# Output projection of a fused recurrence and gated MLP: weights held still, gated tile streamed, sums block-transposed on the way out

## The chip, the cores and the metric

The kernel runs on one NeuronCore of one Trainium2 chip. The metric is the device time of one launch in microseconds, the median of several runs. Five engines matter. TensorE multiplies 128x128 blocks: it loads one operand, the stationary one, into its array, and streams the other, the moving one, past it; the sums land in PSUM. VectorE and ScalarE do elementwise work, GpSimd does almost nothing here, and SyncE's queue issues every DMA. Each engine works through its own instructions in the order in which they were written, and waits on semaphores for the others.

## The reference, cut to what matters

Inputs q, k, v, a_re and a_im have the shape (4, 8, 768, 48): batches, heads, time steps, head dimension. The first half is a linear recurrence with a complex decay per channel, the second a gated MLP over its output:

```python
mag = np.sqrt(a_re * a_re + a_im * a_im)
scale = np.minimum(mag, 0.999) / (mag + 1e-06)
for t in range(S):                                # S_re, S_im: 48x48 states per batch and head
    new_re = ar * S_re - ai * S_im                # ar, ai: a_re, a_im of step t, times scale
    new_im = ar * S_im + ai * S_re
    S_re, S_im = (new_re + kv, new_im)            # kv: outer product of k[t] and v[t]
    y[:, :, t] = einsum('bhd,bhde->bhe', q[:, :, t], S_re)
x = y.transpose(0, 2, 1, 3).reshape(3072, 384)
g = x @ w_gate                                    # 384 x 1536
out = (g * sigmoid(g) * (x @ w_val)) @ w_out      # 1536 x 384
```

The weights arrive as 64-bit floats, everything else as 32-bit floats.

## The kernel before, in words

Tokens are cut into 24 slabs of 128 rows, and two slabs form a group of 256 tokens (12 groups, numbered 0 to 11). For each group `stage_ops` (L364) computes decays and phases of both slabs on ScalarE and VectorE, `slab_ops` (L590) turns the recurrence of a slab into matmuls on keys and queries that were rotated and scaled by these, and `ffn_ops` (L912) runs the gated MLP. From slab 6 on the keys and queries are turned by VectorE's 32x32 block transposes (L637) and brought into place by twelve small DMAs for each slab (L646, tile `T`); `sc` (L679, tile `p_ps`) is the first product of a slab that needs them.

The MLP has 12 steps for each group, one for each 128 columns of the hidden dimension. A step is written `g.f`. `f1` (L927) makes the gate and value columns in PSUM (`p_gv`); `th` (L933, ScalarE) applies silu; `h2` (L938, VectorE) multiplies by the value, giving `sg`, 128 hidden columns by 256 tokens. From group 1 on TensorE works on rounded 32-bit operands, so that each number is split in a high and a low part: `hh` is the rounded `sg`, `hl` what is left (L340). Three products high*high, high*low and low*high make up one. `f1` thus has 18 matmuls with 256 streamed columns each (two matrices, three blocks of the contraction, three products).

`f2` (L961) multiplies by the output weights. Before the change the gated tile is stationary, 128 tokens at a time, and the 384 weight columns stream: two halves of tokens by three products, 6 matmuls of 384 columns, each half summed over the 12 steps in a PSUM tile of its own (`p_po`, one bank each). The sums have tokens on partitions. `oe` (L972) copies each half to SBUF (`ost`), on ScalarE or VectorE as it falls, and `os` (L975) stores it with one DMA of 128 rows. Group 0 differs: it works on unsplit 32-bit numbers.

The weights are turned from 64-bit words into 32-bit floats by three VectorE operations (`c1` to `c3`), then split into high (`c4`, on ScalarE or VectorE) and low (`c5`); `w` in these names stands for the gate and value weights, `o` for the output weights.

The order of all this is made by a planner at build time (`Planner.plan`, L110). Each operation has an estimated cost, a due time, its dependences and the buffers that it holds, and the planner deals the operations out to the engines one after another, by due time and by constants (L32 to L53). What it writes is the order of each engine's instructions; on the chip only semaphores hold. The names in the change are those of the planner's operations: `h2_2.3`, `oe3.0`, `evt010` (eviction of a TensorE transpose), `kl`, `k1`, `k2` (range checks of the weights), `kz`, `km` (range checks of the decays), `tr` (block transposes), `sh` (the twelve DMAs).

Of the kernel before, what the change touches and what calls it, by code (L numbers as in the profile page):

```python
# [33 lines left out]
SWITCH_KEY = 8.903  # L34
RUSH, WARY = 100.0, 8.0
CALM_S, CALM_C, CALM_T, CALM_A, CALM_D = 4.319, 1.268, 0.639, 0.272, 0.3
LATE, WARY2, WARY3, WARY4 = 2.18, 1.96, 1.727, 0.007
STRETCH = 1.757
AHEAD, YIELD, QUEUED = -15.937, 12.575, 8.752
T0, PER, FT, FT0 = 49.251, 22.663, 4.032, 4.936  # L40
LEAD0, LEAD2 = 12.884, 2.091
CONV0, CONVP = 32.474, 43.543
T1 = T0 + 12 * FT0
CK0, CKP = 169.077, 13.465
RCP, SQR = 1, 2

# [3 lines left out]
TURN_OVER, STILL, GATED, INPUT = 128, 96, 16, 16  # L50
HIGH, LOW, WHOLE = 0, 1, 2
SHY = -4.043
POOL_FROM = 9.827  # L53
# [17 lines left out]
class Planner:  # L71
# [29 lines left out]
    def urge(self):  # L101
# [119 lines left out]
def quick(ctx, tc, q, k, v, a_re, a_im, w_gate, w_val, w_out, out, count):  # L221
# [4 lines left out]
    still = ctx.enter_context(tc.tile_pool(name="still", bufs=1))  # L226
    gap = ctx.enter_context(tc.tile_pool(name="gap", bufs=1))
# [22 lines left out]
    still.tile([P, STILL], F32, name="ahead")  # L250
    gap.tile([P, TURN_OVER - STILL], F32, name="behind")
# [3 lines left out]
    def place(nm, f, dtype):  # L255

        pool = still if nm == "w" else work
        return pool.tile([P, 2 * WIDE[nm]], dtype, name=f"w{nm}{f}", tag=f"w{nm}{f}", bufs=1)

    def spare(nm):  # L260
# [4 lines left out]
        return W[nm]  # L265

# [44 lines left out]
    def new(tag, inst):  # L311
# [4 lines left out]
        elif tag in PSUMS:  # L316
            t = psum.tile([P, 512], F32, name="p_" + tag, tag=tag, bufs=2 if tag == "po" else slots[tag])
# [483 lines left out]
    def weight_ops(f):  # L801
        for nm, n, user in (("w", 2 * DM, "f1"), ("o", DM, "f2")):
# [37 lines left out]
            def c4(e, nm=nm, n=n, whole=whole):  # L840
                W.pop((nm, f - 1, WHOLE), None)
                W[nm, f] = place(nm, f - 1, F32R)
                cast(e, W[nm, f][:, 0:n], whole())

            def c5(e, nm=nm, n=n, whole=whole):
                tt(e, W[nm, f][:, n:2 * n], whole(), W[nm, f][:, 0:n].bitcast(F32), ALU.subtract)
# [65 lines left out]
    def ffn_ops(g):  # L912
        t0, step = (T1 + (g - 1) * NF * FT, FT) if g else (T0, FT0)
        for f in range(NF):
# [36 lines left out]
            def f2(e, f=f, I=I):  # L951
                hh, hl, h = (at_.get((x, I)) for x in ("hh", "hl", "sg"))
                products = ((hh, HIGH), (hh, LOW), (hl, HIGH)) if g else ((h, WHOLE),)
                if f == 0:
                    new("po", f"{g}.0")
                    new("po", f"{g}.1")
                for i in range(2):
                    cs = slice(i * P, (i + 1) * P)
                    po = at_["po", f"{g}.{i}"][:, :DM]
                    for j, (l, part) in enumerate(products):  # L960
# [261 lines left out]
```

## Time and profile before

| | us |
|---|---|
| median of 3 runs | 633.49 |
| the runs | 632.08, 633.49, 633.57 |
| the profiled execution's own time | 632.41 |
| its span, from first to last instruction | 630.7 |
| TensorE matmuls busy in it | 599.1 |
| VectorE busy | 502.6 |
| ScalarE busy | 399.3, of this table loads 146.3 |

The granted clock was 0.998 of 2.4 GHz over the span. A busy TensorE in this profile is one that has a matmul in flight: the ends are modelled, so the pace of matmuls is read from the distance of their starts, and idle time from windows and waits.

### The profile page before, as it was taken

How to read it: one execution, taken by the hardware profiler on the slowest of the kernel's cores; microseconds unless marked ns; L12 is line 12 of the kernel's file. 1: busy time of each engine (PE TensorE's matmuls, PEld its weight loads, DVE VectorE, ACT ScalarE, POOL GpSimd, SP SyncE). 2: the span in 40 equal slices, each digit the busy share in tenths (PEclk: the TensorE clock that was granted, in tenths of full speed). 3: DMA queues.
4: the chain of work that ended last, by engine and by line, in shares of the span. 5: the costliest groups of instructions: out<-in, count | busy, mean ns of one | idle time of the engine just before them, and what ended most of it. 6: DMA issues, size and time to landing. Idle time of an engine off the chain costs nothing.

```text
span 630.7 us, 16366 instructions
## 1 busy us (share of the span) xinstructions
PE 599.1 (95%) x6690; PEld 562.8 (89%) x6690; DVE 502.6 (80%) x930; ACT 399.3 (63%) x650; POOL 4.2 (1%) x15
## 2 busy tenths in 40 slices
PE   2779999989899999999999999999999999999996
PEld 1467788979899999999999999999999999999995
DVE  8999999998986978977989869869879958544432
ACT  7864238886776885767876966966966854221211
POOL 2000000000000000000000000000000000000000
PEclk9999999999999999999999999999999999999999
DMA  8899601233655465555365553563553551431200
GB/s 263 239 294 302 201 27 32 65 120 95 156 134 134 119 133 127 130 144 135 88 146 137 140 135 90 133 167 95 131 164 97 138 151 45 128 81 46 76 1 30
DMA packets 155575, 79.91 MB, mean 127 GB/s; under 512 B 116187, under 2 KB 151261, under 8 KB 155494
## 3 DMA queue, kind: packets, MB, share of 16 engines
q1 hardware_dynamic: 155494, 78.80, 46.4%
q8 instruction: 54, 0.88, 0.6%
q14 instruction: 27, 0.22, 0.1%
HBM read 59.83 MB, written 4.78 MB: 102 GB/s over the span
## 4 chain that ended last, share of the span: by engine, by line
PE 76%; DVE 14%; ACT 3%; SPq 3%; issue 2%; DMA 2%; DVEq 0%
PE p_gv L927 39%; PE p_po L961 20%; PE p_py L679 6%; PE p_ps L679 6%; PE p_pm L745 2%; PE p_pm L491 2%; DVE ww L340 2%; SPq L646 2%; PE p_gv L617 1%; ACT L1053 1%; DVE sg L938 1%; DVE ks L340 1%; DVE s L340 1%; DMA re<-in_a_re_dram 1%; ACT s L395 1%
## 5 line engine op out<-in xcount | busy, mean ns | idle before, releaser
L927 PE MATMUL p_gv<-xh,ww 128*128 128x256 f32 x1596 | 303.0, 287 | 4.1 <-DVE sg L938 3.5
L927 PEld LDWEIGHTS p_gv<-xh,ww 128*128 128x128 f32 x1596 | 255.9, 189 | 12.2 <-DVE sg L938 5.7
L927 PE MATMUL p_gv<-xl,ww 128*128 128x256 f32 x726 | 201.2, 277 | 0.0
L1053 ACT ACT_TABLE_LOAD x114 | 146.3, 1283 | 2.1
L933 ACT ACTIVATE sg<-p_gv 128x256 f32<-128x256 f32 x144 | 54.5, 384 | 130.4 <-PE p_gv L927 129.1
L927 PEld LDWEIGHTS p_gv<-xl,ww 128*128 128x128 f32 x726 | 136.3, 188 | 0.1
L961 PE MATMUL p_po<-wo,hh 128*128 128x384 f32 x484 | 125.5, 340 | 0.0
L938 DVE TENSOR_TENSOR sg<-sg,p_gv 128x256 f32<-128x256 f32 x144 | 59.0, 414 | 62.5 <-ACT sg L933 62.3
L961 PEld LDWEIGHTS p_po<-wo,hh 128*128 128x128 f32 x484 | 81.2, 188 | 2.4 <-issue 2.2
L961 PE MATMUL p_po<-wo,hl 128*128 128x384 f32 x242 | 80.8, 334 | 0.0
L340 DVE TENSOR_TENSOR hl<-sg,hh 128x256 fp32r<-128x256 f32 x132 | 54.5, 418 | 5.3 <-ACT hh L344 0.8
L961 PEld LDWEIGHTS p_po<-wo,hl 128*128 128x128 f32 x242 | 45.4, 188 | 0.0
L395 ACT ACTIVATE s<-s 128x768 f32<-128x768 f32 x44 | 37.0, 844 | 11.2 <-DVE s L340 7.2
L679 PEld LDWEIGHTS p_ps<-T 96*64 96x64 f32 x768 | 35.9, 138 | 5.9 <-issue 2.9
L679 PE MATMUL p_ps<-T 96*64 96x128 f32 (+1 forms) x768 | 39.6, 254 | 0.9 <-DVE T L346 0.9
L344 ACT CAST hh<-sg 128x256 fp32r<-128x256 f32 x49 | 19.8, 405 | 22.5 <-DVE sg L938 20.2
L707 DVE TENSOR_TENSOR sc<-p_ps,turn 128x512 f32<-128x512 f32 x48 | 32.0, 687 | 2.5 <-PE p_ps L679 2.1
L346 DVE CAST hh<-sg 128x256 fp32r<-128x256 f32 x83 | 23.8, 289 | 3.7 <-PE p_po L961 0.4
L679 PE MATMUL p_py<-sc,vr 128*32 128x128 f32 x384 | 26.4, 273 | 0.0
L884 ACT ACTIVATE wo<-wo 128x384 f32<-128x384 f32 x36 | 20.1, 560 | 9.0 <-DMA wo<-in_moe_w_gate_dram 6.3
L765 ACT CAST xh<-p_py 128x384 fp32r<-128x384 f32 x22 | 10.5, 479 | 23.4 <-PE p_py L679 23.2
L679 PE MATMUL p_py<-sc,vt 128*32 128x128 f32 x384 | 25.0, 273 | 0.0
(140 smaller groups left out, 853.1 us busy)
## 6 DMA issues: line engine op xcount, KB each, us to landing
T<-ww SPq DMA_DIRECT2D x216, 64.0 KB, 2.9
wo<-in_moe_w_out_dram SPq DMA_DIRECT2D x24, 384.0 KB, 6.1
ww<-in_moe_w_gate_dram SPq DMA_DIRECT2D x12, 384.0 KB, 5.9
vt<-in_v_dram SPq DMA_DIRECT2D x24, 192.0 KB, 4.0
ww<-in_moe_w_val_dram SPq DMA_DIRECT2D x12, 384.0 KB, 6.7
out_dram<-ost SPq DMA_DIRECT2D x24, 192.0 KB, 2.4
wo<-in_moe_w_gate_dram SPq DMA_DIRECT2D x12, 384.0 KB, 3.7
wo<-in_moe_w_val_dram SPq DMA_DIRECT2D x12, 384.0 KB, 3.4
```

Of the source, the lines that this page charges most:

```text
L340: V[e].tensor_tensor(out=out, in0=a, in1=b, op=op)
L344: nc.scalar.copy(out=out, in_=in_)
L346: nc.vector.tensor_copy(out=out, in_=in_)
L395: nc.scalar.activation(out=of(dst), in_=of(source), func=func, scale=scale, **kw)
L679: nc.tensor.matmul(out=o, lhsT=l, rhs=r, start=opens, stop=closes, tile_position=(0, width * slot), skip_group_check=True)
L707: nc.vector.tensor_tensor(out=s.rearrange("p (r m) t -> p r m t", m=2), in0=scores[qd].rearrange("p (r m) t -> p r m t", m=2), in1=m, op=A ...
L884: nc.scalar.activation(out=high(0), in_=high(1), func=AF.Square, accum_out=flags[:, fl_hi + j:fl_hi + j + 1])
L927: nc.tensor.matmul(out=gv[:, i, :], lhsT=l, rhs=r, start=(m == 0), stop=(m == len(mm) - 1))
L933: nc.scalar.activation(out=new("sg", I), in_=at_["gv", I][:, 0:2 * P], func=AF.Silu)
L938: nc.vector.tensor_tensor(out=sg, in0=sg, in1=at_["gv", I][:, 2 * P:4 * P], op=ALU.mult)
L961: nc.tensor.matmul(out=po, lhsT=l[:, cs], rhs=weight("o", f, part), start=f == 0 and j == 0, stop=f == NF - 1 and j == len(products) - 1)
L1053: nc.scalar.preload_act_table_set(op.load)
```

## The change

In groups 1 to 10 `f2` now loads the output weights as the stationary operand, 128 output columns at a time, and streams the whole gated tile, 256 tokens: three blocks of output columns by three products, 9 matmuls of 256 columns. The sums have output columns on partitions and 256 tokens along the row, 768 floats in one PSUM tile of two banks. `oe` turns them back by one VectorE transpose of 32x32 blocks for each slab. A block transpose leaves the four blocks of a column of blocks where they are, so the split of the output weights (`c4`, `c5`) writes their columns in another order (`rows_of`), and the store takes four DMAs for each slab, in runs of 96 floats, where it took one. Groups 0 and 11 (`upright`) keep the former products; group 11 undoes the column order in its copy. The PSUM tile `po` is one tile with two banks instead of two tiles with one. Two padding tiles are gone, and the gated tiles and inputs start 48 floats into their buffers instead of 16. The planner has other constants, and a table that moves single due times.

```diff
-SWITCH_KEY = 8.903
+SWITCH_KEY = 3.7845
+NUDGE = {
+    "sadd0.1": -5.6, "lnr1": 0.2, "cumF1.1": 3.8, "mk1_2": 14.3, "mk1_3": 15.5, "c32w": 4.0, "c110w": 3.4,
...
-TURN_OVER, STILL, GATED, INPUT = 128, 96, 16, 16
+TURN_OVER, GATED, INPUT = 128, 48, 48
...
+        for op in self.ops:
+            op.key += NUDGE.get(op.name, 0.0)
...
+    def rows_of(nm, at, plain=False):
+        if nm != "o":
+            return at
+        return at.rearrange("p (q k m) -> p q k m", k=KT, q=4) if plain else at.rearrange("p (k q m) -> p q k m", k=KT, q=4)
...
-            t = psum.tile([P, 512], F32, name="p_" + tag, tag=tag, bufs=2 if tag == "po" else slots[tag])
+            t = psum.tile([P, 1024 if tag == "po" else 512], F32, name="p_" + tag, tag=tag, bufs=slots[tag])
...
-                cast(e, W[nm, f][:, 0:n], whole())
+                cast(e, rows_of(nm, W[nm, f][:, 0:n]), rows_of(nm, whole(), True))
...
+        upright = g in (0, NGRP - 1)
...
-                    for j, (l, part) in enumerate(products):
-                        nc.tensor.matmul(out=po, lhsT=l[:, cs], rhs=weight("o", f, part),
-                                         start=f == 0 and j == 0, stop=f == NF - 1 and j == len(products) - 1)
...
+                wh, wl = (weight("o", f, x).rearrange("p (k n) -> p k n", k=KT) for x in (HIGH, LOW))
+                for k in range(KT):
+                    for j, (l, r) in enumerate(((wh, hh), (wl, hh), (wh, hl))):
+                        nc.tensor.matmul(out=po[:, 2 * P * k:2 * P * k + 2 * P], lhsT=l[:, k, :], rhs=r,
+                                         start=f == 0 and j == 0 and k != 1, stop=f == NF - 1 and j == 2, skip_group_check=True)
...
-                cast(e, new("ost", I), at_["po", I][:, :DM])
+                    cast(e, *((rows_of("o", x, plain) for x, plain in ((o, True), (part, False))) if g else (o, part)))
+                else:
+                    nc.vector.transpose(out=o.rearrange("p (j k m) -> p k j m", j=4, k=KT),
+                                        in_=po[:, 0:2 * P * KT].rearrange("p (k i j m) -> p k i j m", k=KT, i=2, j=4)[:, :, i])
...
+                for q in range(4):
+                    nc.sync.dma_start(out=r.rearrange("(j a) (q n) -> q a j n", a=32, q=4)[q],
+                                      in_=o[32 * q:32 * q + 32].rearrange("a (j n) -> a j n", j=4))
```

On TensorE, where group 5 ends and group 6 begins, the order before had this, from the last matmul of `f1` 6.2 on (`hh` and `hl` of step 6.0 are stationary, two PSUM tiles):

```order
L927 MATMUL p_gv_4668<-xh_4272,ww1_919 128x256
L961 MATMUL p_po_4698<-wo-1_298,hh_4663 128x384 x2
L961 MATMUL p_po_4698<-wo-1_298,hl_4687 128x384
L961 MATMUL p_po_4699<-wo-1_298,hh_4663 128x384 x2
L961 MATMUL p_po_4699<-wo-1_298,hl_4687 128x384
L927 MATMUL p_gv_4716<-xh_4272,ww2_941 128x256
```

After the change the same place reads (the first operand named is the moving one, `wo` is stationary):

```order
L941 MATMUL p_gv_5598<-xh_5091,ww1_904 128x256
L980 MATMUL p_po_5632<-hh_5594,wo-1_336 128x256 x2
L980 MATMUL p_po_5632<-hl_5596,wo-1_336 128x256
L980 MATMUL p_po_5632<-hh_5594,wo-1_336 128x256 x2
L980 MATMUL p_po_5632<-hl_5596,wo-1_336 128x256
L980 MATMUL p_po_5632<-hh_5594,wo-1_336 128x256 x2
L980 MATMUL p_po_5632<-hl_5596,wo-1_336 128x256
L941 MATMUL p_gv_5648<-xh_5091,ww2_934 128x256
```

Six matmuls of 384 columns have become nine of 256, in the same place between the same two steps of `f1`.

On VectorE, in group 2 (`sg` rows are `h2`, the product by the value columns; `hl` rows the low parts; `ks`, `qs` and the transposes belong to the next slabs), the order before had, from `h2_2.1` on:

```order
L938 TENSOR_TENSOR sg_1860<-sg_1860,p_gv_1802 128x256
L340 TENSOR_TENSOR ks_1871<-kt_1362,s1_1821 128x16x48
L340 TENSOR_TENSOR qs_1601<-qt_1373,s1_1821 128x16x48
L340 TENSOR_TENSOR hl_1902<-sg_1792,hh_1823 128x256
L340 TENSOR_TENSOR ks_1871<-kt_1362,s3_1437 128x16x48
L340 TENSOR_TENSOR qs_1601<-qt_1373,s3_1437 128x16x48
L637 STREAM_TRANSPOSE ww11_1451<-ks_1871 128x4x2x3x32
L938 TENSOR_TENSOR sg_1916<-sg_1916,p_gv_1833 128x256
L637 STREAM_TRANSPOSE ww11_1451<-qs_1601 128x4x2x3x32
L340 TENSOR_TENSOR hl_1948<-sg_1860,hh_1900 128x256
```

and after the change, with the two transposes of group 1's sums (`ost`) around `h2_2.1`:

```order
L996 STREAM_TRANSPOSE ost_1900<-p_po_1091 128x3x4x32
L952 TENSOR_TENSOR sg_1875<-sg_1875,p_gv_1828 128x256
L996 STREAM_TRANSPOSE ost_1908<-p_po_1091 128x3x4x32
L353 TENSOR_TENSOR ks_1932<-kt_1372,s1_1847 128x16x48
L952 TENSOR_TENSOR sg_1910<-sg_1910,p_gv_1879 128x256
L353 TENSOR_TENSOR ks_1932<-kt_1372,s3_1455 128x16x48
L353 TENSOR_TENSOR qs_1616<-qt_1386,s1_1847 128x16x48
L650 STREAM_TRANSPOSE ww11_1467<-ks_1932 128x4x2x3x32
L353 TENSOR_TENSOR qs_1616<-qt_1386,s3_1455 128x16x48
L353 TENSOR_TENSOR hl_1980<-sg_1875,hh_1934 128x256
L650 STREAM_TRANSPOSE ww11_1467<-qs_1616 128x4x2x3x32
L952 TENSOR_TENSOR sg_1995<-sg_1995,p_gv_1912 128x256
```

Between `h2_2.1` and `h2_2.2` there were four products of 768 columns, one `hl` and a transpose of 768; now there are one transpose of 384 and one product of 768. The `hl` of step 2.0 has moved up, ahead of the rows shown.

On SyncE's queue, around slab 10 (`T` rows are the DMAs that bring keys and queries in place, `out_dram` the store of group 3), the order before had:

```order
L646 DMA T<-ww_1451 32x8x64 x3
L668 DMA vr_89<-in_v_dram 64x2x48 x4
L654 DMA vt_87<-in_v_dram 128x8x48
L646 DMA T<-ww_1451 32x8x64 x9
L975 DMA out_dram<-ost 128x384 x2
L537 DMA s_3384<-fr 128x768
```

and after the change:

```order
L659 DMA T<-ww_1467 32x8x64 x3
L681 DMA vr_83<-in_v_dram 64x2x48 x4
L1005 DMA out_dram<-ost 32x4x96 x4
L659 DMA T<-ww_1467 32x8x64 x9
L1005 DMA out_dram<-ost 32x4x96 x4
L550 DMA s_3539<-fr 128x768
```

Four stores stand ahead of the nine `T` DMAs, where one load of `v` stood, which has moved behind them.

## Rows read from the trace of the kernel before

**Rows 1.** The page's first part: busy time, share of the span, instructions.
```profile
PE 599.1 (95%) x6690; PEld 562.8 (89%) x6690; DVE 502.6 (80%) x930; ACT 399.3 (63%) x650; POOL 4.2 (1%) x15
```

**Rows 2.** Windows: stretch, length, busy time of each engine, granted clock, DMA share, GB/s.
```profile
0.00:45.00 45.00, 26.73 (x284) 16.97 (x284) 41.34 (x67) 33.58 (x55) 4.18 (x15) 1.00 0.86 268
45.00:131.00 86.00, 84.42 (x653) 71.09 (x652) 85.93 (x158) 49.14 (x75) 0.00 (x0) 1.00 0.43 121
131.00:175.00 44.00, 39.92 (x518) 36.80 (x516) 41.06 (x66) 34.65 (x56) 0.00 (x0) 1.00 0.47 136
175.00:624.00 449.00, 447.49 (x5237) 437.70 (x5237) 333.67 (x641) 281.50 (x465) 0.00 (x0) 1.00 0.45 114
624.00:630.70 6.70, 0.53 (x4) 0.20 (x2) 0.56 (x1) 0.48 (x1) 0.00 (x0) 0.80 0.20 67
```

**Rows 3.** Chain of work that ended last, 396 to 412 us: start, length, what.
```profile
398.70 2.06 PE p_gv L927 x18
400.76 1.04 PE p_po L961 x6
...
```

**Rows 4.** The chain, 421 to 432 us.
```profile
425.12 0.35 PE p_pm L491 x2
425.47 2.04 PE p_gv L927 x18
...
```

**Rows 5.** Groups by line: names, shapes, count, busy us, mean ns, idle before.
```profile
L1053 ACT ACT_TABLE_LOAD x114 | 146.3, 1283 | 2.1
...
L637 DVE STREAM_TRANSPOSE ww<-ks 128x768 f32<-128x768 f32 x18 | 17.5, 974 | 3.3 <-DMA T<-ww 3.1 <-DMA out_dram<-ost 0.2
...
L346 DVE COPY ost<-p_po 128x384 f32<-128x384 f32 x13 | 7.0, 550 | 1.2 <-PE p_po L961 1.2
...
L346 DVE COPY T<-p_gv 96x512 f32<-96x512 f32 x6 | 4.1, 684 | 0.4 <-PE p_gv L617 0.3
...
L346 DVE CAST ww<-ww 128x768 fp32r<-128x768 f32 x4 | 2.3, 571 | 0.0
```

**Rows 6.** Timeline of VectorE, 163 to 177 us: start, length, instruction.
```profile
165.10 0.41 DVE L938 TENSOR_TENSOR sg<-sg,p_gv 128x256 f32<-128x256 f32 x1
165.43 0.95 DVE L340 TENSOR_TENSOR ks<-kt,s 128x768 f32<-128x768 f32 x1
...
170.13 0.39 DVE L938 TENSOR_TENSOR sg<-sg,p_gv 128x256 f32<-128x256 f32 x1
...
175.02 0.75 DVE L938 TENSOR_TENSOR sg<-sg,p_gv 128x256 f32<-128x256 f32 x2
```

**Rows 7.** Waits of TensorE, 158 to 178 us: total us, times, longest.
```profile
PE p_gv L927 <- DVE sg L938: 2.4, 3, 1.6
```

**Rows 8.** Tile `p_po`, 355 to 360 us: duration min/median/max ns, first and last start.
```profile
L961 PE MATMUL p_po<-wo-1_298,hh x4: 335/338/339, 358.8 to 359.5; 128*128 128x384 f32 x4
...
L961 PE MATMUL p_po<-wo,hl x2: 331/332/333, 356.1 to 356.6; 128*128 128x384 f32 x2
L346 DVE COPY ost<-p_po x2: 549/550/551, 357.3 to 357.7; 128x384 f32<-128x384 f32 x2
```

**Rows 9.** Timeline of SyncE's queue, 258 to 276 us.
```profile
260.08 1.97 SPq L646 DMA_DIRECT2D T<-ww  x3
...
265.50 6.80 SPq L646 DMA_DIRECT2D T<-ww  x9
272.40 1.03 SPq L975 DMA_DIRECT2D out_dram<-ost  x2
```

**Rows 10.** The chain, 272 to 280 us.
```profile
276.71 1.55 PE p_ps L679 x24
```

**Rows 11.** The page's DMA issues: names, count, KB each, median us to landing.
```profile
T<-ww SPq DMA_DIRECT2D x216, 64.0 KB, 2.9
```

**Rows 12.** Timeline of all engines, 622 to 631 us.
```profile
624.04 0.56 DVE L346 COPY ost<-p_po 128x384 f32<-128x384 f32 x1 [1.22 <-PE p_po L961]
...
624.56 0.48 ACT L344 COPY ost<-p_po 128x384 f32<-128x384 f32 x1 [3.06 <-PE p_po L961]
625.07 1.09 SPq L975 DMA_DIRECT2D out_dram<-ost  x2
```

More of the change, by code (lines that the diff above doesn't have):

```diff
@@ L33 @@
 HOP = 0.189
-SWITCH_KEY = 8.903
+SWITCH_KEY = 3.7845
 RUSH, WARY = 100.0, 8.0
-CALM_S, CALM_C, CALM_T, CALM_A, CALM_D = 4.319, 1.268, 0.639, 0.272, 0.3
-LATE, WARY2, WARY3, WARY4 = 2.18, 1.96, 1.727, 0.007
+CALM_S, CALM_C, CALM_T, CALM_A, CALM_D = 4.0404, 0.9631, 0.2445, 0.2607, 0.2775
+LATE, WARY2, WARY3, WARY4 = 2.1401, 1.7581, 1.3142, 0.0
 STRETCH = 1.757
[L39 to L42, printed above, removed]
+AHEAD, YIELD, QUEUED = -15.9216, 13.0405, 5.6794
+T0, PER, FT, FT0 = 49.2709, 22.6488, 4.035, 4.9297
+LEAD0, LEAD2 = 8.0784, 1.9836
+CONV0, CONVP = 33.0252, 40.2957
 T1 = T0 + 12 * FT0
-CK0, CKP = 169.077, 13.465
+CK0, CKP = 169.2028, 13.465
 RCP, SQR = 1, 2
+NUDGE = {
[9 rows of a table added]
+}
 WIDE_KEYS = 64
 TURNS = P // WIDE_KEYS
-TURN_OVER, STILL, GATED, INPUT = 128, 96, 16, 16
+TURN_OVER, GATED, INPUT = 128, 48, 48
 HIGH, LOW, WHOLE = 0, 1, 2
-SHY = -4.043
-POOL_FROM = 9.827
+SHY = -9.7365
+POOL_FROM = 9.8301
 TABLES = {"exp": ("exp_and_others", "natural_log_exp_and_others"), "ln": ("natural_log_exp_and_others",),
@@ L249, in quick @@
     turned_v = [const.tile([P, 2, 2, 64], F32, name=f"vr{i}") for i in range(2)]
-    still.tile([P, STILL], F32, name="ahead")
-    gap.tile([P, TURN_OVER - STILL], F32, name="behind")
     W, HALVES = {}, {}
@@ L255, in place @@
     def place(nm, f, dtype):
-        pool = still if nm == "w" else work
-        return pool.tile([P, 2 * WIDE[nm]], dtype, name=f"w{nm}{f}", tag=f"w{nm}{f}", bufs=1)
+        return work.tile([P, 2 * WIDE[nm]], dtype, name=f"w{nm}{f}", tag=f"w{nm}{f}", bufs=1)
     def spare(nm):
@@ L952, in f2 @@
                 hh, hl, h = (at_.get((x, I)) for x in ("hh", "hl", "sg"))
-                products = ((hh, HIGH), (hh, LOW), (hl, HIGH)) if g else ((h, WHOLE),)
                 if f == 0:
[L955 to L959, printed above, removed]
-                    for j, (l, part) in enumerate(products):
-                        nc.tensor.matmul(out=po, lhsT=l[:, cs], rhs=weight("o", f, part),
-                                         start=f == 0 and j == 0, stop=f == NF - 1 and j == len(products) - 1)
+                    new("po", g)
+                po = at_["po", g]
+                if upright:
+                    products = ((hh, HIGH), (hh, LOW), (hl, HIGH)) if g else ((h, WHOLE),)
+                    for i in range(2):
+                        for j, (l, part) in enumerate(products):
+                            nc.tensor.matmul(out=po[:, 512 * i:512 * i + DM], lhsT=l[:, P * i:P * i + P], rhs=weight("o", f, part),
+                                             start=f == 0 and j == 0, stop=f == NF - 1 and j == len(products) - 1)
+                    return
+                wh, wl = (weight("o", f, x).rearrange("p (k n) -> p k n", k=KT) for x in (HIGH, LOW))
[3 more added lines that the diff above has]
+                                         start=f == 0 and j == 0 and k != 1, stop=f == NF - 1 and j == 2, skip_group_check=True)
             PO = [("po", g)]
```

18 lines of the change are left out of this document (11 added, 7 removed), and 8 rows, old and new, of the table NUDGE.

## Prediction, made before the changed kernel ran

> **What bounds the kernel now.** I read the page's first part, then windows, then the chain of waits inside them, then the groups by line. TensorE has a matmul in flight 95% of the span [rows 1], but the windows show four regimes [rows 2]. Up to 45 us TensorE is busy 26.7 of 45, and VectorE 41.3: the start-up of decays and phases. From 45 to 131 us both are full (84.4 and 85.9 of 86), so there a gain on one is worth something only with the other. From 131 to 175 us TensorE lacks 4.1 us and VectorE 2.9. From 175 to 624 us TensorE is busy 447.5 of 449 while VectorE is idle a quarter of the time: whatever shortens TensorE's instructions there comes off the end one for one, and nothing that VectorE, ScalarE or the queue does matters until TensorE waits for it. The last 6.7 us are the final copy, the store and the closing. The granted clock was 1.00 in the first four stretches [rows 2], the upper level, 2.4 GHz.
>
> **The products, part by part.** One step is 6 x 384 = 2304 streamed columns before and 9 x 256 = 2304 after. At 2.4 GHz that is 0.96 us either way, so only what a matmul costs beyond its columns counts. `f2` takes 1.04 us for 6 matmuls [rows 3], 173 ns each, 13 above the 160 of its columns. `f1` has the form that `f2` gets: 128x128 weights, 256 columns streamed. 18 of them take 2.06 us behind an `f2` [rows 3] and 2.04 behind a 384-column prefix sum [rows 4], 113 to 114 ns, 7 above the 107 of their columns. Nine at that pace are 1.02 (at 2.04) to 1.03 (at 2.06). I take 1.02, a gain of 0.02 for each step. It counts only where TensorE is the bound, from 175 us: ten steps left of group 2 and eight groups of twelve, 106 steps, -2.1 us. The ends: 1.03, so -1.1 us; and if the 0.02 by which `f1` is longer behind an `f2` vanishes too, -4.2.
>
> The Trainium skill speaks against this change: its page "TensorE: Matmul & The Clock Gate", section "Back-to-back issue gap", gives a matmul a gap of its columns divided by the clock plus a fixed 2.5 ns, however many columns it has. Nine then cost 7.5 ns more than six, and 106 steps would add 0.8 us instead of taking 2.1 off. This case's trace disagrees so far: the part beyond the columns is 7 ns at 256 columns and 13 at 384, so it is not fixed.
>
> From rows alone the same fear has a larger size: should each of the nine carry the 13 ns that a matmul of `f2` carries now, a step is 9 x 120 = 1.08, 0.04 longer, +4.2 us. That is a rival below.
>
> Weights that stay and a gated tile that streams also change whom TensorE waits for: the load of weights no longer waits for `hh`, only the matmul does. In the full stretch it hardly waits at all (1.5 us in 449), so I give this nothing. The shifted offsets of tiles in SBUF I also cost at nothing: the trace has no second offset. Their bound is the 7 ns that an `f1` matmul costs beyond its columns, 18 x 7 ns x 106 steps = 13 us either way, which I hold for unlikely: `f1` runs at 2.04 to 2.06 in all the steps shown, with other weight tiles each time [rows 3, 4].
>
> **The order of the start.** Ahead of the first `h2` of group 1, VectorE's order has lost three evictions of transposed tiles (684 ns each) and gained one cast of gate and value weights (571 ns) [rows 5]: -2.05 + 0.57 = -1.5 us. Other moved items are the same instructions in another place. Up to 131 us VectorE is the fuller engine (41.3 of 45 and 85.9 of 86 [rows 2]), so I take the whole 1.5 off. The evictions go to ScalarE, which has 11 us free before 45 and 37 between 45 and 131 [rows 2]; that is their cover. Ends: 0, if TensorE (84.4 of 86) hides it, and -2.05, if the cast falls where VectorE has room.
>
> **Group 2.** In the trace TensorE waits three times for `h2`, 2.4 us in all, between 158 and 178 us [rows 7]. The VectorE rows show why: `h2_2.1` at 165.10, then four products of 0.95 us, and `h2_2.2` only at 170.13; the next two at 175.02 [rows 6]. The change puts `h2_2.2` two operations behind `h2_2.1`, and the low parts sooner. The four products and the transposes do not go away, they come behind, and are late for slab 6 next. I take 1.5 of the 2.4 us off; ends 0 and -2.4.
>
> **What is added.** (1) Each group's sums now leave by two transposes on VectorE, one behind the other, and the next group's first `f2` waits for both, since they empty one PSUM tile. The row for 768 columns is 974 ns; a plain copy of 384 out of PSUM is 550 [rows 5]. A product of 768 columns takes 950 [rows 6], so a transpose is only 24 ns above a plain operation of its size, and I take 0.56 for 384 columns. In the trace of group 5 both copies already ran on VectorE, from 357.3, the second from 357.7 for 0.55, and the next group's first matmul began at 358.8 [rows 8]: 0.5 us to spare. Two of 0.56 fit. But the six halves of before had two tiles, so the first copy could begin half a step earlier, and before each pair something of 0.95 us may stand on VectorE. I take 0.05 for each of ten groups, +0.5; ends 0 and, at 0.97 for each transpose (no faster than 768 columns), 2 x 0.42 - 0.5 = 0.34 each, +3.4. Behind a waiting matmul stand `f1` and all else on TensorE, so it is paid in full.
>
> (2) Stores: 8 DMAs a group where there were 2, at some 0.52 each (1.03 for two), up to 0.66 (1.97 for three small ones) [rows 9]: +3.1 to +4.2 us on the queue for each group. Mostly they stand behind the `T` DMAs of one slab and ahead of the next, which have time. At slab 10 four stores stand ahead of nine `T` DMAs, in place of one load of 0.6: +1.5 to 2.0. In the trace the last of the nine was issued by 272.3, 2.9 us is the median to landing [rows 11], and `p_ps` began at 276.71 [rows 10]: 1.5 us to spare. TensorE is also earlier by then by 3 us, its feeders not surely. I take +0.8 for this slab, nothing for others; ends 0 and 2 us at each of ten groups.
>
> (3) Table loads of ScalarE: the order has 119 where the trace had 114, 1.28 us each [rows 5], 6.4 us on an engine that is free 37% of the time. +0.3; ends 0 and 2.5 (two loads in front of a silu that TensorE needs).
>
> (4) The end. The last group's two copies read one PSUM tile where they read two. VectorE's began at 624.04, before the last matmuls, ScalarE's at 624.56 [rows 12]; now the first must wait for all matmuls, and the second, on ScalarE, for the first. 624.56 + 0.56 + 0.48 = 625.6 instead of 625.04, and the second store follows by as much less what the two stores overlap: +0.4, ends 0.2 and 0.6.
>
> Casts and subtractions of the output weights in another column order stay on the same engines and have the same columns; nothing, their cover being that only a dozen each exist, before 131 us.
>
> **Sum**: -2.1 - 1.5 - 1.5 + 0.5 + 0.8 + 0.3 + 0.4 = -3.1. The profiled execution took 632.41, its span 630.7 and 1.7 around it, which does not change: 629.3. That execution is 1.1 below the median of the runs shown (633.49) and near their lowest; counted from the median it is 630.4. I predict between the two, 629.8.
>
> **Rivals.** A: no change, because half of the gains are covered: nine matmuls take the 1.04 us of the six, or VectorE's 1.5 us at the start and part of group 2 are hidden by a TensorE that is as full. Without the -2.1 the sum is -1.0, without the start and group 2 it is -0.1: 632 to 633. For it: both engines are full from 45 to 131 us. Against it: `f1`'s pace. The fixed gap of the Trainium skill's page "TensorE: Matmul & The Clock Gate" (section "Back-to-back issue gap") would end here too: with +0.8 for -2.1 the sum is -0.2.
>
> B: slower, by the nine matmuls alone. If what a matmul costs beyond its columns goes with loading a fresh stationary operand beside a streamed tile just written (13 ns, as `f2` has it), nine cost 1.08: +4.2 in place of -2.1, sum +3.2, 636. It decides from a step above 1.06. Against it: the 384-column form may owe its 13 ns to its length, and `f1`, which also reloads weights for each matmul, has 7.
>
> C: slower, by the hand-over. At 0.97 for a transpose or with one more 0.95 us operation ahead of each pair, each of ten groups waits 0.35 to 0.9: +3.4 to +9 in place of +0.5, 632 to 638. It decides from 0.5 us a group, beyond the spare time in [rows 8].
>
> D: slower, by the queue: `T` comes late in most groups, 1 us for each of ten in place of the 0.8, 639. It decides where a slab has less than about 2 us to spare. Against it: the 24 `T` DMAs of a group take 24 x 0.66 = 16 us [rows 9] of a queue that has some 47 us for it (449 us for nine and a half groups).
>
> E: better than forecast: the `f1` behind an `f2` also loses its 0.02 us, and all of the start's and group 2's waits go: -4.2 - 2.0 - 2.4 + 2 = -6.6, 626.
>
> **Chances**: forecast 0.46 (627.5 to 631.5), E 0.12, A 0.26, B 0.05, C 0.07, D 0.04. About 0.3% (1.9 us) is what a measurement of this kernel can tell from no change. Faster, under 631.6: forecast and E, 0.58, and a little of A, 0.6. Slower, over 635.4: B, most of C, D, 0.14. Same: 0.26. The range goes from 626 (E's middle) to 634.5 (all of A and the near end of C); what is left out is half of E and most of B, C and D, some 0.2.
>
> **What would show it.** Right: in the chain after 175 us, `f2` pieces of 9 at 1.02 us and steps of 3.06 to 3.08 where 3.10 stood; TensorE 2.5 to 3 us less idle before 175; the transposes at about 0.56 us; no new wait of TensorE for `ost` above 0.3 us. Wrong: `f2` at 1.05 or more; rows of waits that name `ost` or `T`, once in each group; the first `f1` of group 1 no earlier than before.

## The result, and the profile after

The changed kernel took 641.48 us (median of 6 runs, 635.91 to 642.49), the kernel before 633.53 beside it (6 runs, 632.08 to 634.82): ratio 1.0103, 95% interval 1.0079 to 1.0127. Forecast were 629.8 and a range of 626.0 to 634.5. It is slower by 1%, and the prediction was wrong in sign.

The profiled execution took 636.64 us, its span is 634.9 (before 630.7). The page's first part, then windows (stretch, length, busy time of each engine, clock, DMA share, GB/s), which answer to [rows 1, 2]:

```profile
PE 599.6 (94%) x7050; PEld 564.9 (89%) x7050; DVE 504.4 (79%) x932; ACT 403.5 (64%) x653; POOL 4.2 (1%) x15
```

```profile
0.00:45.00 45.00, 26.17 (x283) 17.40 (x284) 40.31 (x66) 34.32 (x57) 4.20 (x15) 1.00 0.86 249
45.00:131.00 86.00, 84.91 (x676) 71.25 (x674) 85.85 (x157) 52.15 (x79) 0.00 (x0) 1.00 0.45 133
131.00:175.00 44.00, 41.63 (x561) 39.33 (x562) 41.14 (x68) 32.63 (x53) 0.00 (x0) 1.00 0.51 132
175.00:624.00 449.00, 442.83 (x5511) 433.44 (x5510) 335.37 (x639) 283.51 (x464) 0.00 (x0) 1.00 0.47 114
```

From 131 to 175 us TensorE is busy 1.7 us more than before, as forecast. From 175 us on it is idle 6.2 us of 449, where it was 1.5: new waits have come into the stretch in which TensorE was the bound.

The chain at two places (start, length, what), to set beside [rows 3]:

```profile
258.45 1.02 PE p_po L980 x9
259.47 2.04 PE p_gv L941 x18
```

```profile
542.14 2.12 PE p_gv L941 x18
544.26 1.06 PE p_po L980 x9
```

One form of matmul has two paces. At 113.3 ns (2.04 / 18) a step takes 3.06 us, as forecast; at 117.8 it takes 3.18, against 3.10 before. Up to 505 us the slow pace comes in stretches of 3 to 15 us, from 509 us to the end it does not stop. Group 11, whose `f2` is the former one, has it too.

TensorE's waits from 175 us on (engine, line, waited for: us, times, longest); before there were 1.5 us for `sg` and nothing else:

```profile
PE p_gv L941 <- DVE sg L952: 4.1, 6, 1.1
PE p_pm L504 <- DVE G L353: 1.9, 1, 1.9
```

The second row is a single place, near 330 us. On SyncE's queue eight stores stand ahead of the load of a range check of the weights (`wo`); VectorE's check (L892) waits for that load, the sum into `G` that empties `p_pm` stands behind the check, and TensorE's next prefix sum (`p_pm`, L504) waits for that. SyncE's queue, then VectorE (start, length, instruction):

```profile
318.52 5.64 SPq L1005 DMA_DIRECT2D out_dram<-ost  x8
...
324.67 0.43 SPq L888 DMA_DIRECT2D wo<-in_moe_w_val_dram  x1
```

```profile
330.23 0.55 DVE L892 TENSOR_REDUCE flags<-wo 128x1 f32<-128x384 f32 x1 [2.37 <-DMA wo<-in_moe_w_val_dram]
330.70 0.54 DVE L353 TENSOR_TENSOR G<-G,p_pm 96x384 f32<-96x384 f32 x1
```

Two runs below keep this order and have fewer stores on this queue, `oldprod_neworder` (one for each slab) and `newprod_poolstores` (on GpSimd's queue). In both this load is issued at 319.1 and TensorE's wait is gone, so the eight stores cause it.

VectorE's transposes (names, shapes, count, busy, mean ns, idle before and what ended it), for [rows 5]:

```profile
L650 DVE STREAM_TRANSPOSE ww<-ks 128x768 f32<-128x768 f32 x18 | 17.5, 975 | 6.3 <-DMA T<-ww 4.2 <-DMA vr<-in_v_dram 1.1 <-DMA out_dram<-ost 1.0
L996 DVE STREAM_TRANSPOSE ost<-p_po 128x384 f32<-128x384 f32 x20 | 10.6, 559 | 0.6 <-PE p_po L980 0.4
```

The end, for [rows 12]: the second copy now starts behind the first.

```profile
628.13 0.56 DVE L359 COPY ost<-p_po 128x384 f32<-128x384 f32 x1 [1.75 <-PE p_po L974]
628.72 0.48 ACT L357 COPY ost<-p_po 128x384 f32<-128x384 f32 x1 [3.66 <-DVE ost L359]
```

I added up the distances of matmul starts in both traces. A distance above 160 ns (256 columns) or 230 (384) counts as a wait, less the pace.

| us | before | after | difference |
|---|---|---|---|
| start of the second matmul of group 1's first `f1` (the first starts 0.42 earlier) | 101.67 | 101.33 | -0.34 |
| matmuls of `f1` and `f2` from there on | 409.74 | 409.42 | -0.32 |
| waits inside `f1` and `f2` | 9.80 | 11.98 | +2.18 |
| the 2802 other matmuls, their waits included | 102.97 | 105.02 | +2.05 |
| from the last matmul's start to the end | 6.52 | 7.12 | +0.60 |

The sum is 4.2, the difference of the spans. The products gain 0.3 us where 2.1 were forecast, and waits cost 4.2. Of the +2.05, 1.9 us are the one wait of `p_pm` above. The other 5 us of the median have no rows in this profile, whose execution is among the two fastest: these two (636.64 and 635.91) have a mean granted clock of 0.996, the other four (641.41 to 642.49) 0.986 to 0.992. How such a loss comes about shows in a second profile (run `again`, below).

### The profile page after: what moved, and what is told of

Read it like the earlier page. It is cut to its first block, busy times and chain, and to the rows that moved or that the text cites. A ratio compares the mean times of both kernels' runs of the same rounds, so it can differ in the third digit from the quotient of the medians.

```text
span 634.9 us, 17155 instructions
## 1 busy us (share of the span) xinstructions
PE 599.6 (94%) x7050; PEld 564.9 (89%) x7050; DVE 504.4 (79%) x932; ACT 403.5 (64%) x653; POOL 4.2 (1%) x15
## 4 chain that ended last, share of the span: by engine, by line
PE 65%; DVE 13%; DMA 7%; ACT 6%; SPq 4%; issue 3%; DVEq 0%; ACTq 0%
PE p_gv L941 34%; PE p_po L980 13%; PE p_py L692 5%; PE p_ps L692 4%; ACT L1084 4%; PE p_po L974 3%; SPq L659 2%; PE p_pm L504 2%; PE p_pm L758 2%; DMA wo<-in_moe_w_val_dram 2%; DMA re<-in_a_re_dram 2%; ACT s L408 1%; DMA ww<-in_moe_w_val_dram 1%; DVE sg L952 1%; DMA T<-ww 1%
## 5 line engine op out<-in xcount | busy, mean ns | idle before, releaser
L980 PE MATMUL p_po<-hh,wo 128*128 128x256 f32 x660 | 119.8, 279 | 0.0
L980 PEld LDWEIGHTS p_po<-hh,wo 128*128 128x128 f32 x660 | 100.7, 188 | 1.8 <-issue 1.8
L980 PE MATMUL p_po<-hl,wo 128*128 128x256 f32 x330 | 91.7, 278 | 0.0
L980 PEld LDWEIGHTS p_po<-hl,wo 128*128 128x128 f32 x330 | 62.2, 188 | 0.0
L892 DVE TENSOR_REDUCE flags<-wo 128x1 f32<-128x384 f32 x36 | 19.6, 544 | 11.9 <-DMA wo<-in_moe_w_val_dram 8.6
```

Source lines behind the costliest of these rows:

```text
L980: nc.tensor.matmul(out=po[:, 2 * P * k:2 * P * k + 2 * P], lhsT=l[:, k, :], rhs=r, start=f == 0 and j == 0 and k != 1, stop=f == NF - 1 an ...
```

## Experiments

Times are medians, each with its ratio to runs of the kernel before on the same chip (632.3 to 632.9 in the five sets) and the 95% interval. The first two theories are ORDER (the planner's new order makes TensorE wait and its clock fall) and PACE (256-column matmuls lose their fast pace after a wait). PACE was then split in RHYTHM (the slow pace stays on because nothing but 256-column matmuls follows) and LAYOUT (the pace goes with the places of the operands in SBUF). QUEUE (the stores hold up the other DMAs of SyncE's queue) came from the transposes' idle time above.

**Order or products.** A repeat, and three kernels that cross order and products. The order was replayed as a list:

```diff
-    order = pl.plan()
+    order = replay(pl)
```

`again`, the changed kernel: 

> The changed kernel once more, for more times and another profile. Its six runs so far lie at 636 (two) and 642 (four), with a mean granted clock of 0.996 and 0.986 to 0.992. Theory ORDER (the planner's new order lets TensorE stand idle longer in the start, 3.9 and 2.1 us at a stretch, and in most runs the clock falls there for a while; later VectorE waits for late range-check loads): both times again, and a profile of a 642 run shows some 10 us more at the 1.2 GHz level, before 131 us. Theory PACE (a stream of 256-column matmuls alone has no slack, and after a short wait goes on at 118 instead of 113 ns): a 642 run has the upper clock but 118 ns almost everywhere.

638.99 us, 1.0108 [1.0090, 1.0126].

`newprod_oldorder`, the changed kernel with the order of before: 

> The new products, transposes and stores, but every engine in the order of the kernel before (the order is replayed; only the copies out of PSUM that ScalarE did are VectorE's transposes now). ORDER: faster than before, 629 to 632, in one cluster of times, waits as before, clock 0.998. PACE: no faster than before, 633 to 637, with stretches at 118 ns.

642.76, 1.0149 [1.0132, 1.0167].

`oldprod_neworder`, the kernel before with the order of the changed one: 

> The old products, copies and stores (one DMA for each slab, ScalarE or VectorE as it was planned), in the order of the changed kernel. ORDER: slower than before, 636 to 641, some runs with a lower mean clock. PACE: 632 to 635, one cluster, no stretch at 118 ns that lasts longer than the first three matmuls behind an f2.

633.77, 1.0033 [1.0013, 1.0052].

`newprod_oldstart`, the changed kernel with the order of before up to the first product of group 1: 

> The changed kernel, but everything that the order before had ahead of the first f1 of group 1 stands in that old order; the rest follows in the new order. ORDER: no run at 642, one cluster at 634 to 637, mean clock 0.996 or more. PACE: the two clusters stay.

636.66, 1.0069 [1.0048, 1.0090].

Order alone costs 0.3%, the products with their transposes, stores and places 1.5% in the order of before, more than either theory had for that kernel. So the planner's new order does not make the change slow; it takes back more than a quarter of the cost (1.5% to 1.1%). The theory ORDER falls as the main cause. What is left of it is the clock: with the old start (`newprod_oldstart`) no run reaches 640 us, as ORDER had it. Windows of `again`, same columns as above:

```profile
38.00:41.00 3.00, 1.62 (x67) 1.21 (x57) 3.00 (x5) 1.07 (x2) 0.00 (x0) 1.00 0.74 123
41.00:46.00 5.00, 3.70 (x10) 3.03 (x11) 4.12 (x7) 1.21 (x2) 0.00 (x0) 0.66 0.93 325
...
230.00:233.00 3.00, 1.10 (x9) 0.78 (x8) 2.06 (x3) 1.13 (x4) 0.00 (x0) 1.00 0.81 197
233.00:238.00 5.00, 5.00 (x32) 5.00 (x31) 2.09 (x7) 3.59 (x6) 0.00 (x0) 0.66 0.48 111
```

TensorE is busy for 1.62 and 1.10 of 3 us, and then the granted clock is 0.66 over the next 5: the lower level, 1.2 GHz, for 3.4 us of them, in which the second time 16 matmuls of 256 columns took 3.4 us instead of 1.8. A wait of 2 us can so be paid almost twice. It need not be: the first profile has the same gap near 39 us (1.08 of 3 us busy) at 1.00 throughout.

**Places in SBUF.** The prediction gave the shifted offsets nothing. `oldprod_newoffsets` is the kernel before with the places of the changed one:

```diff
-TURN_OVER, STILL, GATED, INPUT = 128, 96, 16, 16
+TURN_OVER, GATED, INPUT = 128, 48, 48
...
-    still.tile([P, STILL], F32, name="ahead")
-    gap.tile([P, TURN_OVER - STILL], F32, name="behind")
```

> The kernel before, with only the places of tiles in SBUF taken from the changed kernel (padding tiles gone, gated tiles and inputs 48 floats into their buffers): moving operands begin at byte 64 of 512 instead of 448, gate and value weights at 384 instead of 256. Products, order and stores are those of before. LAYOUT (a matmul's pace of 113.3 or 117.8 ns goes with the addresses of its operands): the last 120 us run at 117.8 as in the changed kernel, f1 2.12 instead of 2.06 us, some 38 steps x 0.08 = 3 us and more in earlier stretches, 636 to 638. RHYTHM (the slow pace stays on because nothing but 256-column matmuls follows): pace of the end 114.2 with f2's 384 columns between, 632.6, no difference.

636.89, 1.0072 [1.0059, 1.0086]: the products untouched, and 4.2 us slower. Its chain:

```profile
542.54 2.12 PE p_gv L921 x18
544.65 1.05 PE p_po L955 x6
```

Three more kernels move one kind of tile each. `oldprod_movedinputs`:

```diff
-TURN_OVER, STILL, GATED, INPUT = 128, 96, 16, 16
+TURN_OVER, STILL, GATED, INPUT = 128, 96, 48, 48
```

> The kernel before, with only the gated tiles and inputs moved 32 floats up in their buffers (byte 64 of 512 instead of 448); the weights stay where they were. If the pace goes with the place of the moving operands: 117.5 ns in the steps from group 1 on, 636 to 637, as with all places of the changed kernel. If it goes with the places of the weights (or with the distance of the two, which this kernel changes and the changed kernel does not): for the weights 632.7 and 114.2, for the distance another pace than either.

`oldprod_movedweights`, the padding tiles gone and `GATED` and `INPUT` left at 16: 

> The kernel before, with only the weights moved (gate and value weights at byte 384 of 512 instead of 256); gated tiles and inputs stay at 448. Moving operands alone cost 4.8 us (117.8 ns a matmul instead of 114.2), all places together 4.2. If the pace goes with the place of the moving operand alone: 632.7 and about 114 ns. If it goes with the distance of moving and stationary operand (192 bytes of 512 in the kernel before, 320 in the one with moved inputs, 64 here): another pace, 635 to 637 where it is the slow one.

`oldprod_wo256`:

```diff
-        pool = still if nm == "w" else work
+        pool = still
```

> The kernel before, with only the output weights, its moving operand in f2, at byte 256 of 512 instead of 384. If places matter for the 384-column matmuls too: f2's 173 to 174 ns or the first matmuls of f1 behind them (117, 122, 116 ns) change, by up to 1 ns on 795 and 9 ns on 3 of 18 matmuls: 630.5 to 635. If only the places of f1's operands matter: 632.7, the same rows.

Bytes are where the tiles start, modulo 512, as the compiled programs have them; `f1` and `f2` are from the chains near 545 us:

| | `ww` | `wo` | `xh` `xl` `hh` `hl` | `f1` + `f2`, us | time | ratio |
|---|---|---|---|---|---|---|
| before | 256 | 384 | 448 | 2.06 + 1.04 | 632.8 | 1 |
| all moved | 384 | 384 | 64 | 2.12 + 1.05 | 636.89 | 1.0072 [1.0059, 1.0086] |
| inputs moved | 256 | 384 | 64 | 2.12 + 1.04 | 637.21 | 1.0076 [1.0062, 1.0090] |
| weights moved | 384 | 384 | 448 | 2.12 + 1.06 | 638.75 | 1.0105 [1.0090, 1.0121] |
| `wo` moved | 256 | 256 | 448 | 2.12 + 1.05 | 635.90 | 1.0062 [1.0049, 1.0076] |

```profile
543.05 2.12 PE p_gv L927 x18
545.17 1.04 PE p_po L961 x6
```

```profile
541.60 2.12 PE p_gv L927 x18
543.72 1.05 PE p_po L961 x6
```

These are the chains of `oldprod_movedinputs` and `oldprod_wo256`. Each of the four moves puts `f1` at 2.12. (All other tiles moved by multiples of 512 bytes.) `oldprod_movedweights` and `oldprod_wo256` came out slower than any range that was given for them. That places matter is shown; by which rule is not: it is not the moving operand alone, and not its distance to the weights, since the last row leaves both operands of `f1` where they were modulo 512 and slows `f1`. The Trainium skill, page "TensorE: Matmul & The Clock Gate", section "Back-to-back issue gap", says that in a stream of weight loads and matmuls the spacing is set by both, and gives the prediction's fixed 2.5 ns for an isolated matmul only; the rows agree that the columns alone don't set it (256 columns at 113.3 or 117.8 ns), but no run shows how places enter.

In the new form the same places are worth less. `newprod_oldoffsets`, the changed kernel with the places of before: 

> The changed kernel with only the places of tiles in SBUF put back: padding tiles as before, gated tiles and inputs 16 floats into their buffers. LAYOUT: the last 120 us run at 113.3 to 114 ns a matmul, steps of 3.06 there instead of 3.18, 38 x 0.12 = 4.5 us less than the changed kernel: 634.5 to 636.5. RHYTHM: 117.8 from about 509 us to the end, as the changed kernel, 639 to 641.

638.07, 1.0081 [1.0051, 1.0110], where `again` had 1.0108. Most steps of the end run at 3.06, but stretches at 117.8 come earlier (432 us, 468 us). Without waits, the mean over its matmuls of 256 columns from group 1 on is 114.6 ns, 114.8 in the changed kernel, 114.3 before. A gain of the places is not shown here.

`newprod_late384`:

```diff
-        upright = g in (0, NGRP - 1)
+        upright = g == 0 or g >= 9
```

> The changed kernel, its order kept, but groups 9 and 10 also take the former products (6 matmuls of 384 columns, two copies, one store each); groups 1 to 8 keep the new ones. RHYTHM: from group 9 on the steps are those of before, 3.10 instead of 3.18, 36 steps (groups 9 to 11) x 0.08 = 2.9 us less: 636 to 637.5, f1 at 2.04 to 2.06 behind the 384-column matmuls. LAYOUT: f1 stays at 2.12 there and f2 takes 1.05, as in group 11 of the changed kernel: 3.17, 24 steps x 0.01, so 639 to 640.5.

638.32, 1.0091 [1.0059, 1.0124]. In these groups `f1` stays at 117.5 ns a matmul: it was not the lack of 384-column matmuls that kept the slow pace on. RHYTHM falls there. `newprod_order_pool_wo256`, the kernel with stores on GpSimd's queue below, and the output weights placed beside the others: 

> The run with new products, order and places of before and stores from GpSimd's queue (638.0), with one more thing: the output weights begin at byte 256 of 512 like the gate and value weights, instead of 384. If the distance of moving and stationary operand sets the pace, both products now have the 192 bytes at which the former f1 ran at 113.3: steps of 3.06 throughout, 3455 matmuls x 0.8 ns = 2.8 us less, 635 to 636. If the slow pace in the new form comes from the lack of 384-column matmuls, nothing changes: 638, with stretches at 117.8.

639.48, 1.0116 [1.0101, 1.0132]: equal distances don't help. Beside the same kernel without this move (1.0079, below) it is 0.4% slower, so places matter in the new form too.

**The stores.** `oldprod_splitstores` is the kernel before with only this:

```diff
+                for q in range(4):
+                    nc.sync.dma_start(out=r[:, 96 * q:96 * q + 96], in_=o[:, 96 * q:96 * q + 96])
```

> The kernel before, with only the stores of groups 1 to 10 cut into four DMAs of 96 columns each, so that SyncE's queue issues 8 a group instead of 2; products, copies, order and places are those of before. QUEUE: VectorE's idle time ahead of the transposes of keys goes from 3.3 to 6 to 8 us, TensorE waits 3 to 6 us more after 175 us, 635 to 638. Otherwise (the queue has room, what waits in the changed kernel is the two transposes of the sums): 632.5 to 633.5.

636.68, 1.0065 [1.0050, 1.0081]: 3.9 us. SyncE's queue, then VectorE and TensorE, from 312 us on (start, length, instruction):

```profile
312.48 1.96 SPq L980 DMA_DIRECT2D out_dram<-ost  x4
314.49 5.88 SPq L646 DMA_DIRECT2D T<-ww  x9
320.47 1.99 SPq L980 DMA_DIRECT2D out_dram<-ost  x4
```

```profile
319.77 0.56 DVE L346 CAST s<-im 128x768 fp32r<-128x768 f32 x1
322.23 0.98 DVE L637 STREAM_TRANSPOSE ww<-ks 128x768 f32<-128x768 f32 x1 [1.89 <-DMA out_dram<-ost]
323.13 0.38 DVE L938 TENSOR_TENSOR sg<-sg,p_gv 128x256 f32<-128x256 f32 x1
```

```profile
321.67 0.34 PE L491 MATMUL p_pm<-re,tri 128*128 128x384 f32 x1
323.56 0.39 PE L927 MATMUL p_gv<-xh,ww 128*128 128x256 f32 x1 [1.55 <-DVE sg L938]
```

The same place before:

```profile
312.64 0.54 SPq L975 DMA_DIRECT2D out_dram<-ost  x1
313.22 5.87 SPq L646 DMA_DIRECT2D T<-ww  x9
```

```profile
320.63 0.98 DVE L637 STREAM_TRANSPOSE ww<-ks 128x768 f32<-128x768 f32 x1
321.54 0.38 DVE L938 TENSOR_TENSOR sg<-sg,p_gv 128x256 f32<-128x256 f32 x1
```

Link by link: four stores for one put the nine `T` transfers 1.3 us later; the next transpose of keys writes the buffer that they read, and waits; `h2` stands behind it on VectorE; `f1` needs the PSUM tile that `h2` frees. TensorE waits 1.55 us. The row of the transpose names a store, but the times of landing say `T`: the last of the nine lands at 321.84, and in five of this run's six such waits the transpose starts 0.28 to 0.39 us behind the landing of the last `T`, whether or not a store lands in between.

`newprod_poolstores`:

```diff
-                    nc.sync.dma_start(out=r.rearrange("(j a) (q n) -> q a j n", a=32, q=4)[q],
+                    nc.gpsimd.dma_start(out=r.rearrange("(j a) (q n) -> q a j n", a=32, q=4)[q],
```

> The changed kernel, its order kept, but the four stores of each slab in groups 1 to 10 are issued from GpSimd's queue instead of SyncE's. QUEUE (eight stores a group hold up the small T transfers, VectorE's transposes of keys wait for the buffer that these read, h2 stands behind them and TensorE behind h2): VectorE's idle time ahead of the transposes of keys falls from 6.3 us towards the 3.3 of before, TensorE waits 2 to 3 us less after 175 us, 636 to 638. RHYTHM or LAYOUT alone: the end stretch is unchanged at 117.8 and so is the time, 639 to 641. If stores from GpSimd are slower to land, only the buffer of the sums could wait for them.

636.92, 1.0068 [1.0050, 1.0086]; VectorE's idle time before the transposes of keys is 4.5 us instead of 6.3, and the 2802 other matmuls, with the wait of `p_pm` gone, are back at 102.75 us.

Now everything put back but the form, step by step. `newprod_order_offsets_pool` has the order and the places of before and GpSimd's stores, `newprod_order_offsets` SyncE's:

> The same, with the stores on SyncE's queue as in the changed kernel: new products, order and places of before. Against the run with new products and the order of before (642.8) only the places differ. LAYOUT: the pace falls to 113.5 to 114.5, 3 to 4 us less, 638 to 640, and VectorE's idle time ahead of the transposes of keys stays at 8.3 us, TensorE's waits for h2 at 7 us. LAYOUT does nothing in the new form: 642 to 643.

> The new products and transposes with three things put back: the order of before, the places of tiles in SBUF of before, and the four stores of a slab issued from GpSimd's queue so that SyncE's holds no more than before. If LAYOUT, QUEUE and ORDER are all that made the changed kernel slower, what is left is the products' own gain, 106 steps x 0.02 to 0.04 = 2.1 to 4.2 us, less what the two transposes in a row cost: 629 to 631. If the form itself costs (VectorE's transposes hold up h2, pace of 117.8 with 256-column streams only), 633 to 636.

`newprod_order_offsets_onestore`:

```diff
-                for q in range(4):
...
+                nc.sync.dma_start(out=r, in_=o)
```

> New products, order and places of before, and one store of 128 whole rows for each slab as before; the four-way rearrangement of columns and rows in the store is left out, so the output is not in the reference's order. Against the run with four stores (641.9) and the one with four stores on GpSimd's queue (638.0): if all that remains is the stores, in the queue and in the DMA engines, VectorE's idle time ahead of the transposes of keys is back at 3.3 us and the time is 631 to 633.5. If the two transposes of the sums and their hand-over hold up h2: 635 to 637, with TensorE waiting for h2 3 us longer than before.

`newprod_onestore_copies`:

```diff
-                    nc.vector.transpose(out=o.rearrange("p (j k m) -> p k j m", j=4, k=KT),
...
+                    cast(e, o.rearrange("p (k n) -> p k n", k=KT),
+                         po[:, 0:2 * P * KT].rearrange("p (k i n) -> p k i n", k=KT, i=2)[:, :, i])
```

> The run with new products, order and places of before and one store a slab (635.2), with the block transposes of the sums replaced by plain copies on the engines that copied before (VectorE or ScalarE); the turning of the sums and their rearrangement are left out, so the output is not the reference's. What is new beside the kernel before is then only nine matmuls for six and one PSUM tile for two. If the two transposes on VectorE make TensorE wait for h2 (1.6 us more than before in the run with transposes): 633 to 634, waits of f1 back to those of before. If the waits come from the products or the single tile of the sums: 635, waits as in the run with transposes.

| order and places of before, with | time | kernel before beside it | difference | ratio |
|---|---|---|---|---|
| nine products, plain copies, one store | 633.15 | 632.88 | 0.3 | 1.0005 [0.9992, 1.0019] |
| and block transposes | 635.16 | 632.30 | 2.9 | 1.0049 [1.0035, 1.0063] |
| and four stores, GpSimd's queue | 638.03 | 632.78 | 5.2 | 1.0079 [1.0064, 1.0095] |
| or four stores, SyncE's queue | 641.87 | 632.78 | 9.1 | 1.0141 [1.0122, 1.0161] |

The rows come from three sets of runs, so they are compared by their differences. The transposes cost 2.6 us, the four stores on SyncE's queue 6.2. The run with GpSimd's queue missed both ranges that were given for it.

VectorE's transposes of keys in the four, top to bottom:

```profile
L841 DVE STREAM_TRANSPOSE ww<-ks 128x768 f32<-128x768 f32 x18 | 17.6, 976 | 2.5 <-DMA T<-ww 1.9 <-DMA out_dram<-ost 0.6
```

```profile
L841 DVE STREAM_TRANSPOSE ww<-ks 128x768 f32<-128x768 f32 x18 | 17.5, 974 | 2.8 <-DMA T<-ww 2.6 <-DMA out_dram<-ost 0.2
```

```profile
L841 DVE STREAM_TRANSPOSE ww<-ks 128x768 f32<-128x768 f32 x18 | 17.6, 975 | 5.8 <-DMA T<-ww 5.8
```

```profile
L841 DVE STREAM_TRANSPOSE ww<-ks 128x768 f32<-128x768 f32 x18 | 17.6, 975 | 7.6 <-DMA out_dram<-ost 4.4 <-DMA T<-ww 3.3
```

In the last row, too, the two long waits put down to stores (1.43 and 2.75 us) end 0.28 and 0.39 us behind the landing of the last `T`.

GpSimd's queue takes the stores out of the way of `T`'s issue, and 3.8 us come back; 2.4 stay. In one stretch both land together, 456 to 463 us (names, count, KB each, median us to landing); at this place before, `T` took 2.9 (the median of [rows 11] too):

```profile
out_dram<-ost POOLq DMA_DIRECT2D x8, 48.0 KB, 3.4
...
T<-ww SPq DMA_DIRECT2D x5, 64.0 KB, 3.8
```

The Trainium skill says so in "DMA: Bandwidth & Descriptors", section "Issuing engines are not separate DMA queues": transfers from any queue run on the same engines and interleave. The idle time of 5.8 us agrees; whether all 2.4 us are that was not tried. Nor was the number of stores told apart from their shorter runs (96 floats instead of 384).

TensorE's waits from 131 us on in the runs with plain copies and with block transposes, both with one store:

```profile
PE p_gv L1132 <- DVE sg L1143: 3.5, 6, 1.7
```

```profile
PE p_gv L1132 <- DVE sg L1143: 4.5, 7, 1.8
...
PE p_po L1171 <- DVE ost L1187: 0.4, 1, 0.4
```

Behind the wait for `ost` the clock falls. Windows of the run with plain copies, then of the one with block transposes (columns as above):

```profile
167.00:170.50 3.50, 1.82 (x16) 1.63 (x15) 3.50 (x6) 3.47 (x6) 0.00 (x0) 1.00 0.50 151
170.50:174.00 3.50, 3.50 (x33) 3.50 (x32) 3.50 (x7) 3.45 (x8) 0.00 (x0) 1.00 0.56 180
```

```profile
167.00:170.50 3.50, 1.39 (x10) 1.13 (x9) 3.50 (x6) 3.19 (x4) 0.00 (x0) 1.00 0.46 139
170.50:174.00 3.50, 3.36 (x16) 3.37 (x17) 3.50 (x7) 3.30 (x6) 0.00 (x0) 0.51 0.61 213
```

With the transposes TensorE is busy 1.39 of the 3.5 us from 167 us on, and the next 3.5 run at 1.2 GHz: 16 matmuls where the copies have 33, some 1.6 us lost (16 matmuls at 214 ns instead of 113). The clock fell here in four of the five profiles with block transposes in the order of before, and neither with plain copies nor in the kernel before. With four stores on SyncE's queue it fell once more, at 330.6, behind the longest of the waits for `T`; that is part of their 6.2 us.

`oldprod_newstart`, the kernel before with the start of the new order, the best version that the runs pointed to: 

> The kernel before with only the start of its order (up to the first product of group 1) taken from the changed kernel; products, stores and places of before. The best version that the runs point to: the first product of group 1 stood at 99.55 us with the whole new order and the former products, and at 101.67 before. If the start is worth that: 630.5 to 631.5. If a fall of TensorE's clock near 40 us, seen in four of six profiles with the new start and in none with the old, takes it back: 632.5 to 634.

633.26, 1.0021 [1.0000, 1.0041]. No version here beats the kernel before.

## Why the prediction was wrong, step by step

**The step that failed most is (2) of what is added, the stores.** It took +0.8 us, with "nothing for others" beyond slab 10. The four-way stores cost 3.9 us on the former products and 6.2 on the new ones (9.1 less 2.9 in the table). I had asked when TensorE needs `T` for `p_ps`, and found 1.5 us to spare. The one who waits first is VectorE, which may not write the next keys into `ww` before `T` has read them. That row was in front of me: in [rows 5] the transposes of keys wait 3.3 us, 3.1 of it for `T`, so where they wait there was no slack at all. In the new order VectorE's range check is a second victim (1.9 us of TensorE near 330). Rival D had the queue right and the victim wrong; that its 639 is near the median of `again` is luck.

**The term -2.1 for `f2`.** 1.02 us came true wherever the pace was 113.3 ns. I took that pace from two pieces of `f1` and held it for the form's own. It is a pace among two, and the mean in the new form is 114.6 to 114.9 ns (115.3 with `wo` moved). With it nine matmuls take 1.03 and `f1` loses 0.01: -0.3 us in the profile of the changed kernel, -1.0 in the one with plain copies (408.73 against 409.74), and in time 1.0005: nothing. That is rival A's half cover. B's 1.08 never came, but the prediction's sign of being wrong, `f2` at 1.05 or more, did: 1.06 in the end stretch, by the slow pace and not by B's fresh operand, since `f1` has the same pace there.

**The offsets at nothing.** As a judgement of that edit it was wrong by 4.2 us on the former products. In the changed kernel the move explains little, by 642.76 against 641.87 and 638.99 against 638.07 some 1 us, with overlapping intervals.

**The hand-over, +0.5.** The transposes last 0.56 us, as taken. In the run with transposes and one store TensorE waits 0.4 us in all for `ost`, so the wait as I priced it was right and rival C, 0.35 to 0.9 in each of ten groups, falls. But the transposes cost 2.6 us: halves that ScalarE copied now stand on VectorE among `h2`, waits for `h2` grow by 1.0 us, and behind the one wait for `ost` the clock falls, which takes some 1.6. The clock had no term in the sum.

**The start, -1.5.** 0.34 us in the first profile. `oldprod_neworder` shows what was meant, the same matmul of group 1 at 99.55 us, and a span of 629.2; but its runs reach 639, and their ratio is 1.0033. The start alone gives 1.0021. The order has a gap of TensorE near 39 us, behind which the clock fell in four of seven profiles with it and in none of 13 with the old start.

**Group 2, -1.5**: 1.7 us in the window, right. **The end, +0.4**: 0.6. **Table loads, +0.3**: there are 119, as forecast, and no wait of TensorE after 175 us names ScalarE; their price was not tried by itself.

What of the five parts is in the changed kernel's 6 to 8 us follows from one sequence of steps, each as a difference from the kernel before beside it: products +0.3, transposes +2.6, stores +6.2, places +1.0, order -3.8 (642.76 to 638.99), together, up to rounding, the 6.4 of `again`. Parts measured in this sequence need not have these sizes in another.

## What to carry to other kernels

Before a queue gets more transfers, look up who waits for the buffer that the delayed transfers read, not only who uses what they bring: a row of idle time that a DMA already ends says that there is no slack. Count equal streamed columns as equal time until a trace shows that the pace of the form is steady over the whole run. An edit that moves tiles in SBUF can be an edit of the matmuls' pace; try it alone. A wait of TensorE can cost more than its length where the clock falls behind it.

## What the runs showed of the hardware that was not expected

A matmul of 256 columns with a weight load each runs at 113.3 or 117.8 ns, with no stall between; the slow pace held for 115 us, and where the tiles lie modulo 512 bytes has a hand in it (128 bytes, all of `f1` 3% slower). In one profile TensorE was busy 1.62 and 1.10 of 3 us, and behind each the clock stood at 1.2 GHz for 3.4 us; behind the like gap in another profile of the same program, 1.08 of 3 us busy, it stayed at 2.4.
